# Top-k attention and an MLP mixer on one core: six tiles by DMA in every pair of heads from the ninth, O scaled by ScalarE in every other, GpSimd taking two tiles instead of three in first groups

## The chip, the cores and the metric

The kernel runs on one core of a Trainium2 chip. The metric is the device time in microseconds (us) of one execution; of several runs the median is given.

## What is computed

The inputs are q, k and v, each 8 batches x 8 heads x 576 rows x 64 columns in f32, and the four weights of a mixer block. Cut to what matters:

```python
scores = scale * q @ k.transpose(0, 1, 3, 2)          # 576 x 576 for each batch and head
kth = np.partition(scores, -32, axis=-1)[..., -32:-31]
scores = np.where(scores >= kth, scores, -1e9)        # the 32 largest of each row stay
attn = softmax(scores)
x = (attn @ v) as 8 x 576 x 512                       # heads side by side
h = np.maximum(x^T @ w_tok1, 0) @ w_tok2              # over the rows, 576 -> 256 -> 576
u = x + h^T
out = u + np.maximum(u @ w_ch1, 0) @ w_ch2            # over the columns, 512 -> 1536 -> 512
```

## The kernel before

The work is cut into 32 units. Unit u is a pair of heads: u = 4 b + p for batch b and pair p, counted from 0, so the ninth pair is unit 8. A pair has 2 x 576 rows of scores. They make nine tiles of 128 rows: tiles 0 to 7 are four blocks of 128 rows for each of two heads, and tile 8 holds the last 64 rows of both heads. Tiles 0 to 3 are the first group (g = 0, scores in `SS0`), tiles 4 to 8 the second (g = 1, `SS1`).

For each group VectorE finds the 32nd largest score of every row, which the program calls the selection: `upper` (L461) takes the larger of the two halves of a row, `split4` (L493) splits that into sorted quarters, four rounds of MAX8 (L510) with MATCH_REPLACE8 (L515) between them draw out the largest eight at a time, and `low_round` (L529) ends it. GpSimd does the other half of the comparisons with integer sums and differences (L467): `both_bits`, `lower_bits`, and, for the first few tiles of a group, the "helped" ones, `next_bits` and `next_low`. Those give the smaller of two quarters, which VectorE else computes itself in the second instruction of `split4` (`hx<-hi`). `HELPED = (3, 4)` says how many tiles of each group GpSimd helps; one tile of the first group is left to VectorE.

Then each tile is masked, exponentiated and transposed, in one of two ways:

- The old way: ScalarE writes U, which is above zero where a score is below the 32nd (`below_act`, L622), TensorE transposes E and U together so that U cancels what is to go (`p_tr`, L637 and L640), and ScalarE copies the result into `pt` (`p_ev`, L660, and `ptail_ev`, L680, for the last 64 columns of two tiles).
- By DMA ("turned" tiles): ScalarE writes a mask (`far`, L606), a DMA issued by GpSimd adds it to the scores in place (`sink`, L613), ScalarE exponentiates two tiles at once into `pb` (L587), and SyncE issues two DMA transposes from `pb` into `pt` (`turn`, L618).

`TURNED = (0, 1, 4, 5)` are turned in every unit, and in units 8, 10, ... 28 also tiles 2 and 3 (`SIX`). Units 30 and 31 turn tiles 0 to 3.

When `pt` is full, TensorE forms O = P V for each of the two heads, 25 matmuls in one PSUM bank (`o_mm`, L705). The last column of O is the sum of the weights. VectorE takes its reciprocal (`rden`, L717), and O is scaled into `xb`: the first head by five ScalarE instructions (`o_ev`, L727), the second by one VectorE instruction (`o_ev_dve`, L736). There is one bank for O, so the matmuls of the second head wait until the first is scaled. These steps of unit u fall into the first group of unit u + 2 on VectorE. The mixer of a batch (L747 to L851) runs on TensorE and ScalarE beside the selection of the next units.

A planner sets the order of the instructions on each engine: every step is a task with a duration, a priority and the buffers that it takes and gives back, and `Plan.order` lists the tasks by a simulated time. The priorities come from the table `RANK`, with further entries for how long a wait is to be expected (`den0_wait` to `den3_wait` for the reciprocals, `t_wait` for the transposes). On the chip each engine works through its list in order, and waits for the others by semaphores. In idle stretches of the plan TensorE gets matmuls without use (`spare`, L296, "filling"). Until 80 us of the plan's time they fill 80% of a gap; from then on 1.2 us of each gap (`REST`) is left out first.

Of the kernel before, what the change touches and what calls it, by code (L numbers as in the profile page):

```python
# [17 lines left out]
FIRST_FROM = 30  # L18
HELPED = (3, 4)
FIRST_HELPED = (0, 4)  # L20
DIVIDED = 1
SIX_HELPED = (3, 4)
SIX_DIVIDED = 1
SPARE = 0.8
PARTS = 3
JOINT = 4
PRE_OF = 12
NUB = 2
RANK = {
    "h2_gap": 1409, "out_gap": 376, "begin_l": -8, "den0_wait": 10, "den1_wait": 12, "den2_wait": 40, "den3_wait": 46, "t_wait": 16,  # L30
    "q_wait": 206, "v_wait": 1272, "pre_mm": -2610, "pre_ev": -135, "rest_mm": -250, "early_mm": 106, "early_ev": 625, "begin_a": 1888,
    "begin": 423, "flags": 27, "rush": -2932, "rush5": 53, "rush6": -6233, "load": -205, "qk_tr": -245, "qk_ev": -396, "st_mm": 2015,
    "st_ev": -508, "keep": 443, "h1_mm": -684, "h1_ev": -162, "ut_mm": -1061, "ut_ev": -874, "out_mm": 9433, "out_ev": 3197,
# [4 lines left out]
    "o_ev1": 215, "z_s_mm": -52, "z_s_ev": -3558, "z_st_mm": -3510, "z_st_ev": 198, "z_exp_u": -1825, "z_exp_t": 77, "z_far": 52,  # L38
    "z_below": 305, "z_sink": 591, "z_p_tr": -413, "z_p_ev": -9, "z_pt_tr": 190, "z_pt_ev": 737, "z_o_mm": 142, "z_o_ev": -93,
    "z_h1_mm": -196, "z_h1_ev": -255, "z_ut_mm": -624, "z_ut_ev": -724, "z_h2_mm": 259, "z_h2_ev": 238, "z_h2t_mm": -665,  # L40
    "z_h2t_ev": -1056, "z_out_mm": -903, "z_out_ev": -61, "z_h2_gap": -89, "z_out_gap": -963,
}
SPARE_US = 0.22
LEAD = 3.0
CALM = (7.0, 10.0)
SETTLED = 80.0
REST = 1.2


# [4 lines left out]
class Plan:  # L54
# [25 lines left out]
    def order(self):  # L80
        free = {t.eng: 0.0 for t in self.tasks}
        ready = {e: [] for e in free}
        slots = {r: [None] * n for r, n in self.bufs.items()}
        nxt = {r: 0 for r in self.bufs}
        freed = {r: [LEAD + (r not in self.early)] * n for r, n in self.bufs.items()}
        for t in self.tasks:
            if t.nd == 0:
                ready[t.eng].append(t)
        running, out, now = [], [], 0.0
        left = len(self.tasks)  # L90
        while left:
            done = [x for x in running if x[0] <= now]
            if done:
                running = [x for x in running if x[0] > now]
                for end, t in done:
                    for key in t.rel:
                        i = slots[key[0]].index(key)
                        slots[key[0]][i] = None
                        freed[key[0]][i] = end
                    for s in t.succ:  # L100
                        s.nd -= 1
                        s.ready = max(s.ready, end + (0.0 if s.eng == t.eng else LAG[t.eng] + s.slack))
                        if s.nd == 0:
                            ready[s.eng].append(s)
            for e in free:
                if free[e] > now:
                    continue
                best = None
                shut = any(x[1].port and x[0] > now for x in running)
                for t in ready[e]:  # L110
                    if t.port and shut:
                        continue
                    if t.ready > now or (best is not None and (best.prio, best.seq) < (t.prio, t.seq)):
                        continue
                    n = {}
                    ok = True
                    for r, *_ in t.acq:
                        i = (nxt[r] + n.get(r, 0)) % self.bufs[r]
                        ok = ok and slots[r][i] is None
                        n[r] = n.get(r, 0) + 1  # L120
                    if ok:
                        best = t
                if best is not None:
                    ready[e].remove(best)
                    if e == "PE" and best.dur > 0.0:
                        idle = [
                            (max(freed[r][i], free[e]), r, i)
                            for r in self.banks
                            for i in range(self.bufs[r])
                            if slots[r][i] is None  # L130
                        ]
                        at, r, i = min(idle) if idle else (now, "", 0)
                        n = int((now - at - (REST if at > SETTLED else 0.0)) * SPARE / SPARE_US)
                        if n > 0:
                            out.append((now, (r, i, n, now)))
                    for key in best.acq:
                        r = key[0]
                        slots[r][nxt[r] % self.bufs[r]] = key
                        nxt[r] += 1
                    free[e] = now + best.dur  # L140
                    running.append((now + best.dur, best))
                    out.append((now, best))
                    left -= 1
            times = [x[0] for x in running if x[0] > now]
            times += [t.ready for e in ready for t in ready[e] if t.ready > now]
            if not times:
                if left and not any(x[0] <= now for x in running):
                    raise RuntimeError("the plan is stuck")
                continue
            now = min(times)  # L150
        self.span = now
        return out
# [10 lines left out]
def kernel(  # L163
# [126 lines left out]
    def spare(r, i, n, at):  # L290
        if CALM[0] < at < CALM[1]:
            return
        wide = w1b[:, 0:2, :].rearrange("p a c -> p (a c)") if at > SETTLED else zeros[:, :]
        w = wide.shape[1]
        for _ in range(n * 512 // w):
            nc.tensor.matmul(  # L296
                out=banks[r][i][:, 0:w], lhsT=(identB if at > SETTLED else zeros)[:, :], rhs=wide, start=True, stop=True
            )
# [594 lines left out]
    for b in range(B):  # L893
        for t in range(NS):
            at = (0, 0) if b == 0 else ((2, 1), (3, 1), (3, 1), (4, 1), (4, 1))[t] if b == 1 else (NPAIR * b - 2 + t // 2, t % 2)
# [17 lines left out]
        return "F2" if i in (2, 3) else "F"  # L913

    def six(u):
        return u >= 8 and u % 2 == 0

    def plan_unit(u):
        b, p = divmod(u, NPAIR)
# [31 lines left out]
        kb, kd, selE, keep, nmx, PTd = {}, {}, {}, {}, {}, {}  # L951
        preE = None
        st["last"] = last
        st["helped"] = SIX_HELPED if six(u) and u < FIRST_FROM else HELPED if u else FIRST_HELPED
        st["turned"] = [i for i in (FIRST_FOUR if u >= FIRST_FROM else SIX if six(u) else TURNED) if not (last and i >= 4)]
        whole = (
# [6 lines left out]
        for g in range(2):  # L963
# [36 lines left out]
            n = 4 + g  # L1000
# [116 lines left out]
        oe, oes = None, []  # L1117
        for hh in range(2):
            wide = last and hh
            div = wide or hh >= 2 - (SIX_DIVIDED if six(u) and u < FIRST_FROM else DIVIDED)  # L1120
            O = ("mps" if wide else "O", u, hh)
            om = add("PE", 0.97, V + R("o_mm", hh), lambda hh=hh: o_mm(st, mst, p, hh, last),
                     deps=[wt["v", b, t] for t in range(NS)] + [None if last else oe] + tails + [PTd[i] for i in range(NTILE) if i == 2 * NT or i % 2 == hh],
                     acq=[O], rel=([("PT", u)] if hh else []) + ([("vb", b)] if hh and p == NPAIR - 1 else []))
            r = add("DVE", 0.1, U - 500, lambda hh=hh: o_den(st, hh), deps=[om], acq=[("den", u, hh)],
                    slack=0.0 if last else 0.02 * RANK["den%d_wait" % (u % 4)])
            if div:
                r = add("FREE", 0.0, 0, lambda: None, deps=[r])
                oe = add("DVE", 0.46, U - 500, lambda hh=hh: o_ev_dve(st, mst, hh, p), deps=[r], rel=[O, ("den", u, hh)])
            else:  # L1130
                oe = add("ACT", 0.98, V + R("o_ev", hh), lambda hh=hh: o_ev(st, mst, hh, p), deps=[r],
                         acq=[("Xb", b)] if p == 0 and hh == 0 else [], rel=[O, ("den", u, hh)])
            oes.append(oe)
# [365 lines left out]
```

## Time and profile before

| | before |
|---|---|
| median of 3 runs | 853.81 us (852.57, 853.81, 855.36) |
| time of the profiled execution | 855.04 us |
| its span, from the first instruction to the last | 853.3 us |
| VectorE (DVE) busy | 825.9 us, 97% of the span |
| ScalarE (ACT) busy | 782.6 us, 92% |
| TensorE (PE) busy | 788.8 us, 92% |
| GpSimd (POOL) busy | 661.1 us, 77% |
| mean granted TensorE clock | 0.993 |

A busy share is the time in which an engine had an instruction under way. Instructions on VectorE overlap by some 0.1 us at their ends, so what one costs in a full stream is read from the start of one to the start of the next.

### The profile page before, as it was taken

Reading aid. Unit: us, or ns where it says so; the run is one execution under the profiler, and the core shown is the slowest. Engines: PE = TensorE matmul, PEld = TensorE weight load, DVE = VectorE, ACT = ScalarE, POOL = GpSimd, SP = SyncE. Lnnn points to the kernel's source line nnn. Section 1 sums busy time; section 2 is a strip of 40 time slices with the busy share of each in tenths; the row PEclk is TensorE's granted clock in tenths of the full one; section 3 lists DMA queues with packets and bytes.
Section 4 is the critical chain, followed back from the end, with each engine's and each line's share of the span. In section 5 each row is a group of like instructions: output and inputs, shape, how many; then the busy total and the mean of one; then the engine's idle time right before and its main releaser. Section 6 shows DMA issues by size and latency. Waiting matters only on the chain. (4 is left out here: it accounts for less than half of the span.)

```text
span 853.3 us, 21743 instructions
## 1 busy us (share of the span) xinstructions
PE 788.8 (92%) x7189; PEld 449.1 (53%) x7189; DVE 825.9 (97%) x3895; ACT 782.6 (92%) x1591; POOL 661.1 (77%) x525
## 2 busy tenths in 40 slices
PE   8999988988999899899989999898998999899996
PEld 6766554644554555455545445555544555455552
DVE  7999999999999999999999999999999999999982
ACT  4589998999999999999999999999999999999972
POOL 8788888878778987888797887789778887877600
PEclk9999999999999999999999999999999999999998
DMA  9358976566685786679665786768775697445521
GB/s 139 74 97 155 146 142 116 98 116 103 133 176 101 141 145 145 117 117 164 151 141 92 131 165 131 154 104 142 150 146 122 109 170 155 107 74 125 133 33 59
DMA packets 234408, 107.08 MB, mean 125 GB/s; under 512 B 217136, under 2 KB 219632, under 8 KB 234288
## 3 DMA queue, kind: packets, MB, share of 16 engines
q0 software_dynamic: 51360, 52.70, 35.1%
q1 hardware_dynamic: 181648, 52.56, 31.1%
q8 instruction: 58, 0.95, 0.5%
q14 instruction: 62, 0.51, 0.2%
q10 hardware_dynamic: 1280, 0.36, 0.2%
HBM read 35.78 MB, written 9.44 MB: 53 GB/s over the span
## 5 line engine op out<-in xcount | busy, mean ns | idle before, releaser
L510 DVE MAX8 A<-hx 128x8 f32<-128x72 f32 (+2 forms) x1152 | 271.7, 299 | 0.0
L515 DVE MATCH_REPLACE8 hx<-A,hx 128x72 f32<-128x72 f32 (+1 forms) x864 | 200.2, 247 | 0.0
L467 POOL TENSOR_TENSOR hi<-sum,hi 128x1152 int32<-128x1152 int32 x64 | 188.8, 2950 | 4.9
L467 POOL TENSOR_TENSOR sum<-SS 128x1152 int32<-128x1152 int32 x64 | 188.1, 2940 | 4.0 <-ACT SS L366 1.6
L360 ACT COPY SS<-s 128x512 f32<-128x512 f32 x379 | 169.2, 503 | 8.4 <-PE s L422 7.3
L467 POOL TENSOR_TENSOR top<-hi,top 128x576 int32<-128x576 int32 (+1 forms) x63 | 78.8, 1251 | 124.9 <-DVE hx L493 124.9
L422 PE MATMUL s<-qkT 64*128 64x512 f32 x508 | 167.2, 644 | 7.7 <-ACT SS L360 7.4
L640 PE MATMUL tp<-identN,U 128*128 128x128 bf16 (+1 forms) x665 | 97.9, 221 | 22.1 <-ACT U L622 22.0
L529 DVE MAX8 A<-hi 128x8 f32<-128x296 f32 x288 | 117.4, 460 | 0.1
L606 ACT ACTIVATE fbuf<-SS,kbig 128x576 uint8<-128x576 f32 x150 | 115.2, 804 | 1.7 <-DVE kbig L598 1.7
L622 ACT ACTIVATE U<-SS,A 128x576 bf16<-128x576 f32 x133 | 106.7, 811 | 1.5 <-PE tp L640 1.5
L637 PE MATMUL tp<-identB,E 128*128 128x128 bf16 (+1 forms) x665 | 102.0, 224 | 0.1
L843 PE MATMUL mps<-wc2b,H2T 128*128 128x512 bf16 (+1 forms) x420 | 101.4, 380 | 0.0
L461 DVE TENSOR_TENSOR hi<-SS 128x1152 f32<-128x1152 f32 x64 | 99.6, 1556 | 1.2 <-ACT SS L360 0.5
L587 ACT ACTIVATE pb<-SS,nmax 128x1152 bf16<-128x1152 f32 x75 | 96.4, 1285 | 0.0
L802 PE MATMUL mps<-UT,wc1b 128*128 128x512 bf16 x336 | 83.8, 380 | 8.1 <-ACT H2T L809 6.2
L587 ACT ACTIVATE E<-SS,nmax 128x1728 bf16<-128x1728 f32 (+1 forms) x52 | 82.2, 1581 | 9.3 <-DVE nmax L554 9.0
L637 PEld LDWEIGHTS <-E 128*128 128x128 bf16 (+1 forms) x665 | 64.7, 100 | 43.5 <-issue 31.0
L640 PEld LDWEIGHTS <-U 128*128 128x128 bf16 (+1 forms) x665 | 66.3, 101 | 32.8 <-ACT U L622 28.2
L467 POOL TENSOR_TENSOR hx<-top,hi 128x576 int32<-128x576 int32 (+1 forms) x63 | 79.7, 1265 | 4.8
L422 PEld LDWEIGHTS s<-qkT 64*128 64x128 f32 x508 | 47.4, 185 | 55.6 <-ACT SS L360 29.5
L705 PE MATMUL O<-vb,pt 128*128 128x65 bf16 x1575 | 66.1, 195 | 10.1 <-DVE hx L515 5.6
(159 smaller groups left out, 1531.0 us busy)
## 6 DMA issues: line engine op xcount, KB each, us to landing
SS<-fbuf POOLq DMA_DIRECT2D x75, 576.0 KB, 5.0
qL<-in_q_dram SPq DMA_DIRECT2D x62, 128.0 KB, 3.6
kL<-in_k_dram SPq DMA_DIRECT2D x60, 128.0 KB, 3.3
out_dram<-ob SPq DMA_DIRECT2D x28, 256.0 KB, 3.0
vb<-in_v_dram POOLq DMA_DIRECT2D x32, 128.0 KB, 5.9
pt<-pb SPq DMA_TRANSPOSE x150, 2.9
wc1b<-in_moe_w_ch_dram POOLq DMA_DIRECT2D x4, 384.0 KB, 6.8
wc2b<-in_moe_w_ch_dram POOLq DMA_DIRECT2D x4, 384.0 KB, 7.3
```

Source lines behind the costliest of these rows:

```text
L360: nc.scalar.copy(out=out, in_=in_)
L422: nc.tensor.matmul(out=x[:, :], lhsT=T[rows[hh], 0, t * P : (t + 1) * P], rhs=T[rows[hh], 1, 0:W], start=True, stop=True,)
L467: nc.gpsimd.tensor_tensor(out=out.bitcast(i32), in0=in0.bitcast(i32), in1=in1.bitcast(i32), op=op)
L510: nc.vector.max(A[:, i, at], hx[:, i, 0:w])
L515: nc.vector.match_replace(hx[:, i, 0:w], A[:, i, TOP[r] : TOP[r] + 8], hx[:, i, 0:w], NEG)
L529: nc.vector.max(A[:, i, KTH : KTH + 8], lists["hi"][:, i, :])
L587: nc.scalar.activation(out=x[:, 0:n, 0:S], in_=st["SS", g][:, a : a + n, :], func=AF.Exp, bias=st["nmax", g][:, 0:1])
L606: nc.scalar.activation(out=mask_buf(i)[:, a % 2, :].bitcast(u8)[:, 1 : 2 * S : 2], in_=srow(st, i), func=AF.Relu, bias=st["kbig", g][:, a ...
L622: nc.scalar.activation(out=U[:, :], in_=srow(st, i), func=AF.Relu, bias=kcol(st, i), scale=-1.0)
L637: nc.tensor.matmul(out=out, lhsT=st["E", i][:, cols], rhs=identB[:, :], start=True, stop=False)
L640: nc.tensor.matmul(out=out, lhsT=st["U", i][:, cols], rhs=identN[:, :], start=False, stop=True)
L843: nc.tensor.matmul(out=ps[0:ss, 0:C], lhsT=terms[x][0], rhs=terms[x][1], start=(x == 0), stop=(x == n - 1),)
```

## The change

Every unit from 8 to 29 now turns six tiles; before, only the even ones did. In these units GpSimd helps two tiles of the first group, not three (the second group keeps four). In the even ones of them ScalarE scales both heads of O; in the odd ones VectorE scales the second, as before. The filling matmuls leave out the 1.2 us only from 170 us of the plan's time on, not from 80. And `RANK` has other numbers throughout, so that the planner writes another order on every engine.

```diff
-SIX_HELPED = (3, 4)
-SIX_DIVIDED = 1
+SIX_HELPED = (2, 4)
+SIX_DIVIDED = 0
...
-    "h2_gap": 1409, "out_gap": 376, "begin_l": -8, "den0_wait": 10, "den1_wait": 12, "den2_wait": 40, "den3_wait": 46, "t_wait": 16,
+    "h2_gap": 1359, "out_gap": 186, "begin_l": 673, "den0_wait": 33, "den1_wait": 8, "den2_wait": 12, "den3_wait": 35, "t_wait": 0,
...
+SPARSE = 170.0
...
-                        n = int((now - at - (REST if at > SETTLED else 0.0)) * SPARE / SPARE_US)
+                        n = int((now - at - (REST if at > SPARSE else 0.0)) * SPARE / SPARE_US)
...
     def six(u):
-        return u >= 8 and u % 2 == 0
+        return u >= 8
...
-            div = wide or hh >= 2 - (SIX_DIVIDED if six(u) and u < FIRST_FROM else DIVIDED)
+            div = wide or hh >= 2 - (u % 2 if six(u) and u < FIRST_FROM else DIVIDED)
```

Counted over the whole program: on VectorE 22 instructions `hx<-hi` of 144 columns become such of 2 x 144, and 11 of 31 scalings (`xb<-O,rden`, L736) go. ScalarE has 22 masks `far` more and 22 U fewer, 22 copies `p_ev` and 11 `ptail_ev` fewer, and 55 pieces of `o_ev` more. TensorE has 220 small transposing matmuls fewer and 60 filling matmuls of 512 columns more (221, before 161); between the O of unit 0 and that of unit 4 stand 106, where 58 stood. GpSimd has 11 `sink` more, and 22 pairs `next_bits` and `next_low` on two tiles, not three. SyncE has 22 DMA transposes more.

Three places of the new order matter below. The line numbers after the change are higher by one. The first is VectorE at the start of the first group of unit 12, where the two reciprocals for the heads of unit 10 (`rden`) stand; `hi`, `top` and `hx` are the lists of the selection. Before:

```order
L461 TENSOR_TENSOR hi<-SS_4707 128x4x288
L598 TENSOR_SCALAR kbig<-A 128x5
L493 TENSOR_TENSOR top<-hi 128x576
L493 TENSOR_TENSOR hx<-hi 128x144
L493 TENSOR_TENSOR hx<-top 128x4x72 x2
L510 MAX A<-hx 128x8 x4
L515 MATCH_REPLACE hx<-A,hx 128x72 x4
L717 RECIPROCAL rden<-O_148 128x5
L554 TENSOR_REDUCE nmax<-A 128x1
```

After the change, at the same place:

```order
L462 TENSOR_TENSOR hi<-SS_4704 128x4x288
L599 TENSOR_SCALAR kbig<-A 128x5
L718 RECIPROCAL rden<-O_148 128x5
L494 TENSOR_TENSOR top<-hi 128x576
L494 TENSOR_TENSOR hx<-hi 128x2x144
L494 TENSOR_TENSOR hx<-top 128x4x72 x2
L511 MAX A<-hx 128x8 x4
L516 MATCH_REPLACE hx<-A,hx 128x72 x4
L718 RECIPROCAL rden<-O_148 128x5
L555 TENSOR_REDUCE nmax<-A 128x1
```

The first reciprocal has moved ahead of `split4`, the second to where the first stood (before, it comes after the third round), and `hx<-hi` is on two tiles.

The second place is VectorE at the end of the same group, where the second head of unit 10 is scaled before. Before:

```order
L510 MAX A<-hx 128x8
L717 RECIPROCAL rden<-O_148 128x5
L529 MAX A<-hi 128x8
L520 TENSOR_REDUCE hi<-A 128x2x8
L529 MAX A<-hi 128x8 x3
L736 TENSOR_TENSOR xb_124<-O_148,rden 128x5x64
```

After:

```order
L511 MAX A<-hx 128x8
L530 MAX A<-hi 128x8
L521 TENSOR_REDUCE hi<-A 128x2x8
L530 MAX A<-hi 128x8 x3
L462 TENSOR_TENSOR hi<-SS_4869 128x5x288
```

The scaling is gone, so the last MAX8 of the group stands directly ahead of the `upper` of the second group. In the odd units the scaling is there, but ahead of the first L529 (before, in 22 units of the program it is the last instruction of the group; after the change in none).

The third place is TensorE between the matmuls for the two heads of unit 3, with the filling matmuls (`mps<-w1b,identB`). Before:

```order
L705 MATMUL O_148<-vb_114,pt_121 64x65
L381 MATMUL tp_144<-identF,qL 128x64
L381 MATMUL tp_144<-identF,kL 128x64
L296 LDWEIGHTS identB
L296 MATMUL mps_149<-w1b,identB 128x512
```

After:

```order
L706 MATMUL O_148<-vb_114,pt_121 64x65
L352 MATMUL tp_143<-identF,kL 128x128 x4
L382 MATMUL tp_144<-identF,qL 128x64
L382 MATMUL tp_144<-identF,kL 128x64
L397 MATMUL s_145<-qkT 128x64
L397 MATMUL s_146<-qkT 128x64
```

The filling pair stands seven times in a row there before, and nothing else follows until the second head; after the change more work of unit 6 (L352, L397) and six filling pairs stand between the two heads, and seven further pairs follow the second.

More of the change, by code (lines that the diff above doesn't have):

```diff
@@ L29 @@
 RANK = {
-    "h2_gap": 1409, "out_gap": 376, "begin_l": -8, "den0_wait": 10, "den1_wait": 12, "den2_wait": 40, "den3_wait": 46, "t_wait": 16,
-    "q_wait": 206, "v_wait": 1272, "pre_mm": -2610, "pre_ev": -135, "rest_mm": -250, "early_mm": 106, "early_ev": 625, "begin_a": 1888,
-    "begin": 423, "flags": 27, "rush": -2932, "rush5": 53, "rush6": -6233, "load": -205, "qk_tr": -245, "qk_ev": -396, "st_mm": 2015,
-    "st_ev": -508, "keep": 443, "h1_mm": -684, "h1_ev": -162, "ut_mm": -1061, "ut_ev": -874, "out_mm": 9433, "out_ev": 3197,
[4 rows of a table removed]
[L38 to L41, printed above, removed]
+    "h2_gap": 1359, "out_gap": 186, "begin_l": 673, "den0_wait": 33, "den1_wait": 8, "den2_wait": 12, "den3_wait": 35, "t_wait": 0,
+    "q_wait": 732, "v_wait": 815, "pre_mm": -654, "pre_ev": -600, "rest_mm": -515, "early_mm": -7, "early_ev": -5, "begin_a": 374,
+    "begin": -433, "flags": 477, "rush": -1878, "rush5": -706, "rush6": -3498, "load": -223, "qk_tr": 259, "qk_ev": 123, "st_mm": -7,
+    "st_ev": 131, "keep": 77, "h1_mm": 601, "h1_ev": -122, "ut_mm": 442, "ut_ev": 11, "out_mm": 20918, "out_ev": 410, "h2_mm": -19,
[4 rows of a table added]
+    "z_s_mm": 589, "z_s_ev": 950, "z_st_mm": -162, "z_st_ev": 421, "z_exp_u": -268, "z_exp_t": 172, "z_far": 258, "z_below": 171,
+    "z_sink": -331, "z_p_tr": -317, "z_p_ev": 201, "z_pt_tr": -84, "z_pt_ev": 522, "z_o_mm": 210, "z_o_ev": -36, "z_h1_mm": 111,
+    "z_h1_ev": 945, "z_ut_mm": 372, "z_ut_ev": -47, "z_h2_mm": -59, "z_h2_ev": -5805, "z_h2t_mm": -57, "z_h2t_ev": 18,
+    "z_out_mm": -107, "z_out_ev": -626, "z_h2_gap": -59, "z_out_gap": -961,
 }
```

8 rows, old and new, of the table RANK are left out of this document.

## The prediction

> **What bounds the kernel now.** I read the page's first part, then the window of 200 us in the middle of the program. In a windows row stand the stretch, its length, the busy times of TensorE, its weight loads, VectorE, ScalarE and GpSimd, then granted clock, DMA share and GB/s.
>
> ```profile
> PE 788.8 (92%) x7189; PEld 449.1 (53%) x7189; DVE 825.9 (97%) x3895; ACT 782.6 (92%) x1591; POOL 661.1 (77%) x525
> ```
>
> ```profile
> 400.00:600.00 200.00, 185.74 (x1673) 103.42 (x1670) 199.73 (x967) 194.35 (x401) 163.60 (x127) 1.00 0.72 137
> ```
>
> VectorE is busy for 199.73 of 200 us; ScalarE, next, has 5.65 us to spare. Third, the waits of VectorE between 200 and 790 us (us in total, times, longest):
>
> ```profile
> DVE hi L461 <- ACT SS L360: 0.5, 1, 0.5
> DVE rden L717 <- PE O L705: 0.2, 1, 0.2
> ```
>
> That is 0.7 us in 590. So VectorE's own list sets the time of this stretch: what leaves the list is gained, what is added is lost, and what the other engines do counts only where it makes VectorE wait. Fourth, VectorE's timeline (start, duration, what) over two units:
>
> ```profile
> 386.34 1.34 DVE L461 TENSOR_TENSOR hi<-SS 128x1152 f32<-128x1152 f32 x1
> ...
> 388.39 0.30 DVE L493 TENSOR_TENSOR hx<-hi 128x144 f32<-128x144 f32 x1
> 388.61 0.82 DVE L493 TENSOR_TENSOR hx<-top 128x288 f32<-128x288 f32 x2
> 389.35 0.19 DVE L717 RECIPROCAL rden<-O 128x5 f32<-128x5 f32 x1
> ...
> 395.73 0.48 DVE L736 TENSOR_TENSOR xb<-O,rden 128x320 bf16<-128x320 f32 x1
> 396.12 0.47 DVE L529 MAX8 A<-hi 128x8 f32<-128x296 f32 x1
> 396.58 1.21 DVE L529 MAX8 A<-hi 128x8 f32<-128x296 f32 x3
> 397.83 1.66 DVE L461 TENSOR_TENSOR hi<-SS 128x1440 f32<-128x1440 f32 x1
> ...
> 411.17 1.35 DVE L461 TENSOR_TENSOR hi<-SS 128x1152 f32<-128x1152 f32 x1
> ...
> 421.01 1.21 DVE L529 MAX8 A<-hi 128x8 f32<-128x296 f32 x3
> 422.12 0.49 DVE L736 TENSOR_TENSOR xb<-O,rden 128x320 bf16<-128x320 f32 x1
> 422.51 1.66 DVE L461 TENSOR_TENSOR hi<-SS 128x1440 f32<-128x1440 f32 x1
> ...
> 435.86 1.35 DVE L461 TENSOR_TENSOR hi<-SS 128x1152 f32<-128x1152 f32 x1
> ```
>
> Instructions overlap at their ends, so a cost is the distance from one start to the next. The first unit, from 386.34 to 411.17, takes 24.83 us, the second, to 435.86, 24.69. They differ in where the scaling L736 stands. In the second it is the last of the group: three MAX8 from 421.01 to 422.12 are 0.37 each, L736 to `upper` is 0.39. In the first, `upper` follows the MAX8 directly: three from 396.58 to 397.83 take 1.25, where 3 x 0.37 is 1.11. So `upper` of the second group stalls 0.14 us behind a MAX8, and L736 in between hides that.
>
> **The change, part by part.** *Scalings.* Eleven L736 leave VectorE: 11 x 0.39 = -4.3 us.
>
> *Wider `hx<-hi`.* With two helped tiles VectorE takes 22 instructions of 2 x 144 columns for such of 144. The narrow one costs 388.61 - 388.39 = 0.22. The width of 288 is in the next row: two of them from 388.61 to 389.35 are 0.37 each. Hence 22 x 0.15 = +3.3 us. (Bounds: 0, if the engine's fixed part were all, and 22 x 0.22 = +4.8, if width were all; I take the row with the same width and operation.)
>
> *The stall of `upper`.* Over the program, L736 was last in 22 groups and is now last in none (the second place of the order): 22 x 0.14 = +3.1 us. Bounds: 0, if the order now hides the stall in some other way, and +3.1. I take the upper end, since the second place shows MAX8 and `upper` adjacent.
>
> *ScalarE.* The rows of the groups (busy us, mean ns, idle before) and five pieces of `o_ev` in the timeline:
>
> ```profile
> L606 ACT ACTIVATE fbuf<-SS,kbig 128x576 uint8<-128x576 f32 x150 | 115.2, 804 | 1.7 <-DVE kbig L598 1.7
> L622 ACT ACTIVATE U<-SS,A 128x576 bf16<-128x576 f32 x133 | 106.7, 811 | 1.5 <-PE tp L640 1.5
> L660 ACT ACTIVATE pt<-tp 128x512 bf16<-128x512 f32 x106 | 64.9, 629 | 0.8 <-PE tp L640 0.8
> ```
>
> ```profile
> 417.04 1.09 ACT L727 ACTIVATE xb<-O,rden 128x64 bf16<-128x64 f32 x5
> ```
>
> The eleven odd units swap two U for two masks (22 x (811 - 804) ns, nothing) and lose 22 copies of 0.63, -13.9 us (the eleven smaller `ptail_ev`, which go too, I leave out). The eleven even ones gain five pieces each: 11 x 1.09 = +12.0. Together -1.9 us, with 5.65 of 200 free already, so ScalarE does not become the bound and I cost it at 0. If that cover were gone, the price would be the 1.09 us of an even unit, 11 times.
>
> *GpSimd, DMA, TensorE.* The next rows are the mask's DMA and the transposes:
>
> ```profile
> L613 POOL DMA_DIRECT2D SS<-fbuf x75 | 65.1, 877 | 5.9 <-ACT fbuf L606 5.4 <-ACT pt L664 0.3 <-ACT SS L360 0.2
> ```
>
> ```profile
> SS<-fbuf POOLq DMA_DIRECT2D x75, 576.0 KB, 5.0
> pt<-pb SPq DMA_TRANSPOSE x150, 2.9
> ```
>
> Eleven `sink` of 0.88 are 9.6 us for GpSimd, which is idle for 36.4 of 200 and has one tile of `next_bits` and `next_low` less in 22 groups. SyncE issues 22 transposes more. A tile by DMA is thus 5.0 + 2.9 us on its way after issue, where O is formed more than a unit later; behind these issues on the queues stand loads for later units. TensorE loses 220 transposes and gets 60 fillings. All off VectorE's list: 0. Their cover is the distance to the reciprocals, and if it is gone, the second rival below is the price.
>
> *The reciprocals come earlier.* They wait for O, and behind them the whole list of VectorE waits. In the trace of before (timelines of VectorE and TensorE, next unit):
>
> ```profile
> 440.23 0.18 DVE L717 RECIPROCAL rden<-O 128x5 f32<-128x5 f32 x1
> ```
>
> ```profile
> 441.61 1.05 PE L705 MATMUL O<-vb,pt 128*128 128x65 bf16 x25 [1.08 <-DVE hx L515]
> ```
>
> From the first reciprocal over the scaling to the end of the second head's matmuls are 441.61 + 1.05 - 440.23 = 2.43 us. Before, the second reciprocal stands two rounds behind the first. In the new order of an even unit the second stands at the old place of the first, 440.23 - 435.86 = 4.37 us into the unit (0.15 more with the wider `hx<-hi`), and the first right behind `upper` (1.35) and `kbig`: some 3.0 us apart by estimate from these rows, so 0.6 us of slack are left. The first one stands 3 us earlier than before in the even units; if it waits, the whole list waits with it. Against waiting at the first one speaks that O of that head needs nothing of VectorE. Bounds: -0.2 (the one listed wait of before goes) and 22 x 0.2 = +4.4, if each new pair waits as that one did. I take 0, near the lower end, as 0.6 us are left.
>
> *Filling from 80 to 170 us.* The only large loss of VectorE in the trace after the start lies here (windows; timelines of TensorE and VectorE):
>
> ```profile
> 140.00:145.00 5.00, 3.41 (x35) 1.76 (x33) 5.00 (x34) 4.51 (x12) 4.76 (x4) 1.00 1.00 183
> 145.00:150.00 5.00, 5.00 (x20) 2.01 (x20) 5.00 (x13) 4.00 (x8) 3.89 (x3) 0.54 0.72 143
> ```
>
> ```profile
> 143.00 1.06 PE L705 MATMUL O<-vb,pt 128*128 128x65 bf16 x25 [1.59 <-ACT xb L727]
> ```
>
> ```profile
> 160.54 1.34 DVE L461 TENSOR_TENSOR hi<-SS 128x1152 f32<-128x1152 f32 x1
> 166.50 0.20 DVE L717 RECIPROCAL rden<-O 128x5 f32<-128x5 f32 x1 [1.51 <-PE O L705]
> 186.85 1.35 DVE L461 TENSOR_TENSOR hi<-SS 128x1152 f32<-128x1152 f32 x1
> 212.65 1.33 DVE L461 TENSOR_TENSOR hi<-SS 128x1152 f32<-128x1152 f32 x1
> ```
>
> TensorE idles 1.59 us before 143.00 between the two heads (the third place), the granted clock falls to 0.54, TensorE runs late, and the reciprocal at 166.50 holds VectorE for 1.51 us. The two units take 26.31 and 25.80 us, together 2.6 more than 24.69 + 24.83. After the change more work and filling stand in that gap: -2.6 us, with bounds 0 and -2.6. I take the full loss, because the clock is at 1.00 in the window ahead of the gap and at 0.54 behind it. The Trainium skill ("TensorE: Matmul & The Clock Gate", section "HAM oscillation — how this bites in real kernels") speaks against this term: it counts as harmful only idle gaps longer than about 3.4 us. The 1.59 us here are shorter and are followed by a lower clock, so trace and rule differ; by the rule filling would bring 0, which is the first rival. Its next section, "A second HAM failure mode: psum-queue depth-cycling", lets frequent short gaps do the same, which would go with the row.
>
> *The end.* Behind VectorE's list TensorE is the limit:
>
> ```profile
> 814.00:826.00 12.00, 11.55 (x153) 7.67 (x152) 9.83 (x22) 7.93 (x22) 0.00 (x0) 1.00 0.30 29
> ```
>
> Of 12 us it is idle for 0.45, so hardly more than that can be gained here by another order: between 0 and -0.45 I take -0.3, since VectorE's list at the end stays nearly as it was and only TensorE's changes.
>
> **Sum.** -4.3 + 3.3 + 3.1 + 0 - 2.6 - 0.3 = -0.8. Against the profiled execution's own 855.04 us that is 854.2. The median shown is 853.81, and its runs spread over 2.79 us, about the size of the clock's loss; if the median execution lost less of it than the profiled one, the change gives back less. So 854.2 stands 0.05% above the median. A measurement of this kernel can tell about 0.3%, or 2.6 us, from no change (851.2 to 856.4): I forecast no measurable change.
>
> **The rivals.** *The loss of clock stays or has another cause.* For it: the gap is short, and the other terms touch nothing there. Against it: the order of events in the rows above. The sum without -2.6 is 856.8, slower by 0.35%.
>
> *Slower: VectorE waits at the earlier reciprocals.* One mechanism: in the 22 units from 8 to 29 O of a head is not ready when its reciprocal's turn comes, at 0.2 us a unit as in the row of waits, +4.4, so 858.6. It decides from (856.4 - 854.2) / 22 = 0.10 us a unit. For it: the slack shrinks to 0.6 us, and the transposes come through 7.9 us of DMA. Against it: 0.6 us is not nothing, and in 590 us of before such a wait is listed once.
>
> *Faster: `upper` does not stall.* If the 0.14 us belong to something other than the MAX8 ahead of it, +3.1 falls away: 851.1, a gain of 0.3%. For it: the row of `upper` shows no idle time. Against it: the two units compared above differ by exactly that.
>
> **How the numbers follow.** The forecast has a chance of 0.57, the clock's loss staying 0.14, waits at the reciprocals 0.14, no stall 0.15. The predicted time is the first one's. The range goes from the no-stall case, 851.0, to just above the first rival, 857.2; outside lie the case of waits and part of the spread around the no-stall one, some 0.2. Faster by over 0.3% is the no-stall case, 0.15; slower are both slower rivals, 0.28; within 0.3% the rest, 0.57.
>
> **What the profile after would show.** Units of 24.6 us where both heads are scaled by ScalarE (24.69 - 0.39 + 0.15 + 0.14 = 24.59) and of 24.98 in the odd ones (24.69 + 0.15 + 0.14); MAX8 to `upper` of the second group at 0.51 everywhere; the wide `hx<-hi` at 0.37; granted clock 1.00 from 140 to 155 us and no wait of VectorE near 166; no idle time ahead of L718 (the reciprocal's line then). The forecast is wrong if `rden` waits for O add up to more than 2 us, if the clock falls somewhere again, or if a unit's length is off by over 0.1 us with no wait listed.

## The result: 9.3 us slower, and the profile after

| | before | after |
|---|---|---|
| median of six runs each | 853.43 us (852.57 to 855.36) | 862.69 us (860.18 to 865.96) |
| ratio, 95% interval | | 1.0112 (1.0092 to 1.0131) |
| time of the profiled execution | 855.04 | 864.72 |
| its span | 853.3 | 863.0 |

The change makes the kernel 1.1% slower; the forecast was 854.2 (range 851.0 to 857.2) and no measurable change. Its runs fall into two groups, three at 860.2 to 860.7 and three at 864.7 to 866.0 us; the profiled execution is of the upper group.

The page's first part, after:

```profile
PE 781.1 (91%) x6931; PEld 443.1 (51%) x7017; DVE 828.6 (96%) x3884; ACT 784.4 (91%) x1613; POOL 660.0 (76%) x536
```

VectorE's busy time has grown by 2.7 us, the span by 9.7. VectorE's timeline over an undisturbed even unit (from 517.55) and an odd one (from 542.16):

```profile
517.55 1.38 DVE L462 TENSOR_TENSOR hi<-SS 128x1152 f32<-128x1152 f32 x1
518.88 0.23 DVE L718 RECIPROCAL rden<-O 128x5 f32<-128x5 f32 x1
518.98 0.76 DVE L494 TENSOR_TENSOR top<-hi 128x576 f32<-128x576 f32 x1
519.64 0.47 DVE L494 TENSOR_TENSOR hx<-hi 128x288 f32<-128x288 f32 x1
520.01 0.83 DVE L494 TENSOR_TENSOR hx<-top 128x288 f32<-128x288 f32 x2
522.10 0.20 DVE L718 RECIPROCAL rden<-O 128x5 f32<-128x5 f32 x1
...
527.50 1.24 DVE L530 MAX8 A<-hi 128x8 f32<-128x296 f32 x3
528.84 1.66 DVE L462 TENSOR_TENSOR hi<-SS 128x1440 f32<-128x1440 f32 x1
...
542.16 1.37 DVE L462 TENSOR_TENSOR hi<-SS 128x1152 f32<-128x1152 f32 x1
...
567.22 1.38 DVE L462 TENSOR_TENSOR hi<-SS 128x1152 f32<-128x1152 f32 x1
```

The even unit takes 24.61 us (24.59 were forecast), the odd one 25.06 (24.98). The wide `hx<-hi` costs 520.01 - 519.64 = 0.37, as forecast. Neither early reciprocal waits here. So VectorE's list is nearly what the prediction said; the lost time lies elsewhere. The waits of VectorE from 200 to 790 us, where before 0.7 us were listed in all:

```profile
DVE rden L718 <- PE O L706: 6.0, 3, 5.0
DVE hi L462 <- ACT U L623: 0.5, 1, 0.5
DVE hi L462 <- ACT SS L361: 0.5, 1, 0.5
```

One wait for O took 5.0 us, in unit 15, which is 30.18 us long. It is followed back through five views. First the DMAs issued from 374 to 376.5 us (KB each, median us to landing):

```profile
SS<-fbuf POOLq DMA_DIRECT2D x1, 576.0 KB, 11.8
qL<-in_q_dram SPq DMA_DIRECT2D x2, 128.0 KB, 4.9
vb<-in_v_dram POOLq DMA_DIRECT2D x1, 128.0 KB, 4.3
qL<-in_q_dram SPq DMA_DIRECT2D x1, 32.0 KB, 8.1
pt<-pb SPq DMA_TRANSPOSE x1, 12.0
```

Then the timelines of ScalarE, TensorE and VectorE, with the idle time in front in brackets:

```profile
387.68 1.25 ACT L588 ACTIVATE pb<-SS,nmax 128x1152 bf16<-128x1152 f32 x1 [3.61 <-DMA SS<-fbuf]
```

```profile
389.80 4.05 PE L423 MATMUL s<-qkT 64*128 64x512 f32 x6 [3.85 <-ACT SS L361]
```

```profile
395.52 0.20 DVE L718 RECIPROCAL rden<-O 128x5 f32<-128x5 f32 x1 [5.03 <-PE O L706]
```

And windows of 3.41 us (length; busy PE, PEld, DVE, ACT, POOL; granted clock, DMA share, GB/s):

```profile
384.79:388.20 3.41, 1.16 (x8) 0.33 (x5) 3.41 (x10) 0.52 (x1) 2.29 (x1) 1.00 1.11 172
388.20:391.61 3.41, 1.81 (x4) 0.66 (x4) 2.29 (x6) 3.41 (x7) 0.72 (x1) 0.50 0.54 99
391.61:395.02 3.41, 3.41 (x25) 1.64 (x23) 0.00 (x0) 3.23 (x7) 2.61 (x4) 0.50 1.05 217
```

A mask DMA and a transpose issued at the same time, 375.9 us, take 11.8 and 12.0 us, not 5.4 and 3.0 (the medians); a second transpose, 1.3 us later, takes 11.3. Four loads had been issued in the 2.3 us before. ScalarE stands for 3.61 us with score copies queued behind the waiting exponentiation, so TensorE stands for 3.85. Its clock falls to 0.50 for three windows of 3.41 us, six score matmuls take 4.05 us, O comes late, and VectorE, the engine that sets the time, loses 5.03 us.

### The profile page after: what moved, and what is told of

It reads as the page before. It is cut to its first block, busy times and chain, and to the rows that moved or that the text cites. A ratio compares the mean times of both kernels' runs of the same rounds, so it can differ in the third digit from the quotient of the medians.

```text
span 863.0 us, 21374 instructions
## 1 busy us (share of the span) xinstructions
PE 781.1 (91%) x6931; PEld 443.1 (51%) x7017; DVE 828.6 (96%) x3884; ACT 784.4 (91%) x1613; POOL 660.0 (76%) x536
## 4 chain that ended last, share of the span: by engine, by line
DVE 40%; PE 22%; ACT 14%; issue 5%; DMA 3%; SPq 0%; DVEq 0%; ACTq 0%
DVE A L511 11%; DVE hx L516 9%; DVE hi L462 5%; DVE A L530 5%; PE mps L844 4%; PE s L423 4%; ACT pb L588 4%; DVE hx L494 3%; PE O L706 3%; PE mps L803 3%; DVE top L494 3%; ACT SS L361 2%; ACT fbuf L607 2%; ACT U L623 2%; DMA SS<-fbuf 1%
## 5 line engine op out<-in xcount | busy, mean ns | idle before, releaser
L468 POOL TENSOR_TENSOR top<-hi,top 128x576 int32<-128x576 int32 (+2 forms) x63 | 73.2, 1162 | 106.0 <-DVE hx L494 106.0
L607 ACT ACTIVATE fbuf<-SS,kbig 128x576 uint8<-128x576 f32 x172 | 131.5, 802 | 0.2 <-DVE kbig L599 0.2
L641 PE MATMUL tp<-identN,U 128*128 128x128 bf16 (+1 forms) x555 | 81.1, 220 | 19.5 <-ACT U L623 19.0
L614 POOL DMA_DIRECT2D SS<-fbuf x86 | 73.6, 874 | 32.0 <-ACT fbuf L607 30.8
L803 PE MATMUL mps<-UT,wc1b 128*128 128x512 bf16 x309 | 78.1, 384 | 17.9 <-ACT UT L793 7.4
L638 PE MATMUL tp<-identB,E 128*128 128x128 bf16 (+1 forms) x555 | 85.6, 223 | 0.9 <-ACT SS L361 0.4
L623 ACT ACTIVATE U<-SS,A 128x576 bf16<-128x576 f32 x111 | 84.4, 791 | 0.5
L516 DVE MATCH_VALUE_LOAD hx<-A,hx 128x8 f32 x864 | 82.2, 95 | 0.0
L588 ACT ACTIVATE E<-SS,nmax 128x1728 bf16<-128x1728 f32 (+1 forms) x41 | 67.2, 1642 | 13.0 <-DVE nmax L555 12.9
L706 PEld LDWEIGHTS <-pt 128*128 128x128 bf16 (+1 forms) x1600 | 60.7, 101 | 33.0 <-issue 25.4
L468 POOL TENSOR_TENSOR hx<-top,hi 128x576 int32<-128x576 int32 (+2 forms) x63 | 72.6, 1152 | 4.9
```

The costliest lines, as they stand in the source:

```text
L468: nc.gpsimd.tensor_tensor(out=out.bitcast(i32), in0=in0.bitcast(i32), in1=in1.bitcast(i32), op=op)
L516: nc.vector.match_replace(hx[:, i, 0:w], A[:, i, TOP[r] : TOP[r] + 8], hx[:, i, 0:w], NEG)
L588: nc.scalar.activation(out=x[:, 0:n, 0:S], in_=st["SS", g][:, a : a + n, :], func=AF.Exp, bias=st["nmax", g][:, 0:1])
L607: nc.scalar.activation(out=mask_buf(i)[:, a % 2, :].bitcast(u8)[:, 1 : 2 * S : 2], in_=srow(st, i), func=AF.Relu, bias=st["kbig", g][:, a ...
L638: nc.tensor.matmul(out=out, lhsT=st["E", i][:, cols], rhs=identB[:, :], start=True, stop=False)
L803: nc.tensor.matmul(out=ps[:, 0:W], lhsT=wc1b[:, cc, fc * P : (fc + 1) * P], rhs=mst["UT"][:, cc, 0:W], start=(cc == 0), stop=(cc == NC - 1),)
```

## The clock goes by stretches of 3.41 us

In every profile here the granted clock at any moment is 1.00 or 0.50 (a window's figure is the mean over it), and each stretch of 0.50 in the middle of a program is 3.41, 6.83 or 10.24 us long. A second example needs no late DMA. Unit 10 after, windows and TensorE's timeline:

```profile
255.09:258.50 3.41, 1.38 (x8) 0.48 (x5) 3.41 (x23) 3.41 (x6) 3.33 (x2) 1.00 0.04 9
258.50:261.91 3.41, 3.41 (x15) 1.63 (x14) 3.41 (x12) 2.64 (x8) 3.39 (x6) 0.50 0.44 87
```

```profile
257.64 2.77 PE L803 MATMUL mps<-UT,wc1b 128*128 128x512 bf16 x8 [2.03 <-ACT H2T L810]
```

TensorE is busy for 1.38 of 3.41 us, in its longest gap idle for 2.03, and the next 3.41 us run at 0.50. The table lays such a grid over all fourteen profiles (before, after and the versions below), from the start of a half-clock stretch on, and counts TensorE's busy share in each stretch at full clock between 35 and 830 us:

| busy share of a 3.41 us stretch | stretches | half clock in the next one |
|---|---|---|
| under 0.45 | 22 | 22 |
| 0.45 to 0.52 | 35 | 11 |
| 0.52 to 0.80 | 338 | 7 |
| over 0.80 | 2789 | 0 |

A grid laid a few ns otherwise moves one or two stretches between the rows. The share within a stretch thus tells far more than the length of one gap: in the run with the filling alone (below) five gaps of 1.85 us, at a share of 0.46, were followed by full clock. But it doesn't tell all. Seven stretches with a share of 0.52 and more were followed by half clock, and one of them, from 142.0 us on at 0.71, is the loss in the profile of before on which the prediction's filling term rests. What decides there stays open.

The grid lies otherwise in each execution, so a gap that is cut in two by it can do nothing in one and halve the clock in the next. Near 500 us the changed kernel's two profiles have the same least share of some 3.41 us, 0.48, and the clock falls in one alone. Between 80 and 790 us the places where TensorE is busy for less than half of some 3.41 us number 5 before the change and 14 after it.

## The experiments

**The changed kernel again**, with no edit.

> The changed kernel once more, with a profile. Its six executions fall into two groups, three at 860.2 to 860.7 us and three at 864.7 to 866.0. Theory A (a rare collision of DMAs): the upper group has one long stall, in the profiled execution 5.5 us at the reciprocal of unit 15, behind a mask DMA that took 11.8 us; an execution of the lower group has no mask DMA over 8 us and no wait of VectorE for O over 1 us, and is about 4 to 6 us shorter. Rival (the stall belongs to the order): the mask DMA of unit 15 takes over 11 us again in any execution, and VectorE waits there again for 5 us.

866.22 us, so of the upper group again. The mask DMA near 375.7 took 10.4 us, and VectorE waited 3.6 us for O in unit 15. The two DMAs thus meet again at the same place; but the same profile has half clock near 500 and 690 us too, and 0.7 us lost in unit 20 and 2.4 us in unit 27. The second of these has the same start as in unit 15: a mask DMA issued at 679.6 us took 9.2 us, and ScalarE waited 1.0 us for it. In the first profile the mask of that place, in the same order, took 4.9 us and nothing was lost. Theory A's lower group was not seen here. The rival is right that unit 15 stalls again, with 10.4 and 3.6 us for its 11 and 5.

**Only the filling of the change, on the kernel before.**

```diff
-n = int((now - at - (REST if at > SETTLED else 0.0)) * SPARE / SPARE_US)
+n = int((now - at - (REST if at > SPARSE else 0.0)) * SPARE / SPARE_US)   # SPARSE = 170
```

> The kernel before with only the filling matmuls between 80 and 170 us changed (the 1.2 us left out only from 170 us on). Theory of the prediction: units 6 and 7 take 24.7 and 24.8 us without the half clock from 145 us on, and the median goes down by up to 2.6 us (850.8 to 853). Rival (the clock's loss is of that one execution and mostly absent): within 1 us of before. Second rival: filling delays useful matmuls, slower by over 1 us.

852.70 us (852.00 to 853.51) against 853.25 beside it, ratio 0.9987 (0.9976 to 0.9997): 0.1% faster than before, at the edge of what can be told. The windows that showed the clock's loss:

```profile
140.00:145.00 5.00, 4.53 (x41) 2.51 (x41) 5.00 (x32) 4.58 (x11) 4.82 (x3) 1.00 1.02 185
145.00:150.00 5.00, 5.00 (x48) 2.88 (x47) 5.00 (x13) 5.00 (x11) 3.75 (x3) 1.00 1.12 135
```

TensorE is busy for 4.53 us in the first, not 3.41, and the clock stays at 1.00. Unit 6 takes 24.70 us, not 26.31; unit 7 25.28, not 24.8, since its second `upper` waits 0.5 us as in the trace of before. The forecast's mechanism holds; its 2.6 us were those of an execution that had this loss, and the median gives back 0.55.

**The filling of before, in the changed kernel** (`SPARSE = 80`; 169 filling matmuls of 512 columns, not 221, all other instructions in the same order).

> The changed kernel with the filling matmuls of before (1.2 us left out from 80 us on). If the change's filling is not what costs time, it stays within 1.5 us of the changed kernel's lower group (859 to 862) or gets slower by up to 2.6 us by a half clock near 145 us; if the filling delays units 3 to 9, it is 1 to 2 us faster than 860.

865.69 us (862.48 to 875.98), ratio 1.0180 (1.0111 to 1.0248). Three of its four executions, 862.48 to 867.02, can't be told apart from the changed kernel's; the fourth took 875.98. The profile has half clock at 118, 258, 558 and 749 us. The change's filling isn't what costs time. The profile also settles a point of the run before: from 170 us on its order is that of the changed kernel, but here the mask of unit 15, issued at 375.7 us, took 5.7 us, and unit 15 is 25.06 us long without a wait. So the order brings the DMAs together there, but they aren't slow in each execution.

**Only the new order, on the kernel before** (`RANK` of the change, everything else of before).

> The kernel before with only the new table RANK: the same work on every engine, other order. Theory B (the order costs): units 6 to 11 and 30 show VectorE waiting for score copies of ScalarE as in the changed kernel (0.4 us each in units 6 to 9, 1.1 and 1.8 us in 11 and 30), and the time is 856 to 860. Theory A (the work costs: masks and transposes in odd units): no such waits, 852 to 855.

895.12 us, ratio 1.0477 (1.0449 to 1.0505), far beyond both expectations. The waits of VectorE from 200 to 800 us:

```profile
DVE rden L717 <- ACT SS L360: 14.7, 4, 3.7
DVE rden L717 <- PE O L705: 4.8, 5, 2.6
```

The table can't be judged apart from the work that it orders; so the order's share in the loss stays open in this form, and the next runs keep the order as it is.

**Filling everywhere, in the changed kernel.**

```diff
-SPARSE = 170.0
+SPARSE = 1000.0
```

> The changed kernel with filling matmuls in the whole program as they are up to 170 us (464 of 512 columns, not 221); the order of all other instructions on every engine is the same. Theory C (gaps of TensorE that the plan foresees halve its clock, and then O comes late for the earlier reciprocals): no granted clock under 0.95 near 255, 500 and 690 us, no wait of VectorE for O over 0.3 us outside of unit 15, and 857 to 860. Theory A (only the collision of DMAs near 376 us makes the stalls): the dip at 385 to 400 us and 4 to 5 us of wait in unit 15 stay, 860 to 865. Rival: fillings delay matmuls that VectorE waits for, slower than 863.

856.70 us (855.87 to 858.90), ratio 1.0041 (1.0025 to 1.0057): 6.0 of the 9.3 us are gone, with no instruction moved but fillings. The two windows of unit 15 and unit 10:

```profile
384.79:388.20 3.41, 3.41 (x20) 1.47 (x18) 3.41 (x12) 3.41 (x7) 3.12 (x5) 1.00 0.17 35
...
255.09:258.50 3.41, 2.14 (x10) 0.75 (x10) 3.41 (x27) 3.41 (x4) 3.33 (x2) 1.00 0.00 0
```

No clock under 0.97 is left from 30 to 830 us, no place with TensorE busy for less than 0.63 of 3.41 us, and no wait of VectorE for O is listed from 200 to 790 us. Theory C holds, at slightly less than its 857 to 860. Unit 15 takes 25.26 us; but its mask took only 5.5 us in this execution, so the profile doesn't show what filling does when that mask is slow. The profiled execution, at 858.38 above the median, still loses 1.5 us in unit 12, and this comes from slow DMAs at full clock: a mask and two transposes issued from 298.2 us on took 8.8, 9.0 and 9.1 us, ScalarE waited 2.48 us for them, its score copies and with them GpSimd's `sum` came late, and `upper` beside that `sum` took 2.63 us.

**Small masks, in the changed kernel** (16 of 128 partitions, so most of the masking is left out).

```diff
-out=st["SS", g][:, a - 1 : a + 1, :], in_=mask_buf(i)[:, :, :]
+out=st["SS", g][0:16, a - 1 : a + 1, :], in_=mask_buf(i)[0:16, :, :]
```

> The changed kernel in which each mask DMA moves 16 of the 128 partitions only (most of the masking is left out; instructions and their order are the same). Theory A (masks that collide with transposes and loads make ScalarE wait, TensorE idle, the clock halve and O late): the wait of ScalarE for the mask near 384 us and the 4 to 5 us in unit 15 go, and the time is 857 to 860 in all executions. Theory C (foreseen gaps of TensorE): dips at 255, 500 or 690 us stay and the time goes down by at most the stall of unit 15. Rival (neither: the loss lies in the list and the late score copies): still 860 and more, with units 6 to 11 and 30 long as before and no stall.

858.82 us (858.38 to 859.44), ratio 1.0065 (1.0048 to 1.0082), with little spread. The mask of unit 15 now:

```profile
SS<-fbuf POOLq DMA_DIRECT2D x1, 72.0 KB, 3.9
```

Unit 15 takes 25.06 us, and the wait of ScalarE is gone; half clock at 259 and 747 us stays. So both theories are right in part: the meeting of DMAs makes the largest stall and most of the spread, the gaps of the plan the rest.

**Both together.**

> The changed kernel with both: mask DMAs of 16 partitions (most of the masking is left out) and filling matmuls in the whole program. Filling alone took 6.0 us off the changed kernel, small masks alone 3.9. If the masks' DMAs cost time only through TensorE's clock, the two don't add: 855.5 to 857, as with filling alone. If they also cost time of their own (late masks, late O), they add further: 853 to 855.

856.19 us (855.45 to 857.35), ratio 1.0029 (1.0019 to 1.0039), within the spread of filling alone. Beside filling, the masks' DMAs thus cost 0.5 us in the median. This doesn't show that they cost time only by way of TensorE's clock: unit 12 with filling, above, speaks against it, and so does unit 15 with three helped tiles and filling, below.

**Filling everywhere on the kernel before** (438 filling matmuls, not 161).

> The kernel before with filling matmuls in the whole program (438, not 161), all else in the same order. The kernel with filling to 170 us alone showed no clock under 0.97 any more and 852.7 us, so if filling only works through the clock, nothing is left to gain: 852 to 853.3. If units 10, 14, 18, 22, 26, whose first reciprocal waits 0.2 us for O, wait for a TensorE that is late by fillings, they get longer: up to 856.

852.74 us, ratio 0.9991 (0.9981 to 1.0001), like 214 of them. With no clock to win back, more filling does nothing, good or bad.

**No filling after 80 us on the kernel before** (`REST = 1000`, 13 filling matmuls left, all else in the same order).

> The kernel before without the filling matmuls after 80 us (13 of 161 of 512 columns are left), all other instructions in the same order. Theory C (a 3.41 us stretch in which TensorE is busy for less than about half is followed by half clock, and O then comes late): half clock in several places, waits of VectorE for O of 1 us and more, 855 to 862. Rival (the old order has slack enough, and fillings matter only to the new one): one or two stretches of half clock, but within 1.5 us of before.

873.90 us (873.05 to 875.70), ratio 1.0233 (1.0215 to 1.0250): 20 us slower with 148 useless matmuls fewer, well beyond the 855 to 862 of theory C. The granted clock in 40 slices, and the waits of VectorE from 80 to 790 us:

```profile
PEclk9999877999999899899989999799998999899999
```

```profile
DVE rden L717 <- PE O L705: 17.9, 14, 2.0
```

So the kernel before too stands next to this edge, held off it by its fillings.

**Three helped tiles, in the changed kernel**, without and with filling everywhere.

```diff
-SIX_HELPED = (2, 4)
+SIX_HELPED = (3, 4)
```

> The changed kernel with three helped tiles in the first groups, as before the change, so that hx<-hi is narrow again on VectorE and GpSimd has more to do. By the prediction's term VectorE's list gets shorter by 22 x 0.15 = 3.3 us, even units 24.45 and odd ones 24.90 us, and without other effects the time is 3 us under the changed kernel's (857 to 859.5). Rival: the mask's issue on GpSimd then comes later behind the longer next_bits, masks land later, and stalls take back more than 3 us: 862 and more.

> The changed kernel with filling in the whole program and three helped tiles in first groups. Without clock losses the prediction's term can be seen by itself: hx<-hi at 0.22, not 0.37 us, 22 x 0.15 = 3.3 us off VectorE's list, so 853 to 854 against 856.7 with filling alone. Rival (GpSimd's longer next_bits holds VectorE or the mask DMAs): units 24.7 and over 25.1 us as in the version with three helped tiles without filling, 857 or more.

869.32 us, ratio 1.0173 (1.0123 to 1.0222), and with filling 866.46, 1.0136 (1.0109 to 1.0162): both rivals. `hx<-hi` is narrow again, and yet units get longer. GpSimd and VectorE in unit 17 of the version with filling:

```profile
437.09 2.63 POOL L468 TENSOR_TENSOR sum<-SS 128x1152 int32<-128x1152 int32 x1 [1.25 <-ACT SS L361]
```

```profile
438.58 2.35 DVE L462 TENSOR_TENSOR hi<-SS 128x1152 f32<-128x1152 f32 x1
```

and the same with two helped tiles and filling:

```profile
435.11 2.63 POOL L468 TENSOR_TENSOR sum<-SS 128x1152 int32<-128x1152 int32 x1
```

```profile
437.89 1.34 DVE L462 TENSOR_TENSOR hi<-SS 128x1152 f32<-128x1152 f32 x1
```

Where the score copies come late, GpSimd's `sum` (437.09 to 439.72) lies beside VectorE's `upper`, which then takes 2.35 us, not 1.34. With filling this happens in units 13, 17, 21, 25 and 29, for 5.7 us together. About as much goes to waits for O from 200 to 790 us:

```profile
DVE rden L718 <- PE O L706: 5.9, 5, 3.4
```

Two of them, 1.7 us in unit 15 and 3.4 in unit 23, follow masks that took 10.0 and 10.3 us. In unit 15 the clock is 1.00 throughout: ScalarE waited 1.36 us for the mask, and O came late without half clock. The order on the other engines differs too in these two versions, so the loss isn't put down to the third helped tile itself.

**VectorE scales the second head in even units too**, with filling everywhere.

```diff
-(u % 2 if six(u) and u < FIRST_FROM else DIVIDED)
+(1 if six(u) and u < FIRST_FROM else DIVIDED)
```

> The changed kernel with filling in the whole program, and the second head scaled by VectorE in even units too (11 L736 more). By the prediction's terms VectorE's list grows by 11 x 0.39 = 4.3 us where L736 stands inside the group, and by 11 x (0.39 - 0.14) = 2.8 where it is the last of the group: 859 to 861 against 856.7. Rival (ScalarE's five pieces in even units delay score copies, and without them GpSimd's sums come in time): less than 2 us slower, or faster.

872.27 us, ratio 1.0213 (1.0196 to 1.0230). VectorE in unit 22:

```profile
571.85 1.35 DVE L462 TENSOR_TENSOR hi<-SS 128x1152 f32<-128x1152 f32 x1
579.80 0.49 DVE L737 TENSOR_TENSOR xb<-O,rden 128x320 bf16<-128x320 f32 x1
...
596.85 1.35 DVE L462 TENSOR_TENSOR hi<-SS 128x1152 f32<-128x1152 f32 x1
```

25.00 us against 24.61 with filling alone: a scaling inside the group costs 0.39 us, the term as forecast. Most of the other 11 us come from units 12, 17, 20 and 30, each 1.5 to 4.2 us longer than its neighbours of the same kind or than with filling alone, and from the end (73.7 us from the start of unit 31, not 70.3), with half clock at 311 and 512 us in spite of the fillings. The planner wrote another order there, so they aren't the price of the scalings.

## Why the prediction was wrong

*What bounds the kernel: right, but not all.* VectorE's list sets the time as long as nothing makes it wait. What the prediction missed is that two things close by make it wait: TensorE's clock, by its busy share per 3.41 us, and DMAs that are slow where they meet.

*Scalings, wider `hx<-hi`: right.* 0.39 and 0.37 us were measured.

*The stall of `upper`: right in kind, somewhat larger.* Three MAX8 to `upper` are 528.84 - 527.50 = 1.34 us, where 3 x 0.37 is 1.11: 0.23, not 0.14. The idle time in front of `upper` is in the lines: 0.10 us here (528.84 - 527.50 - 1.24), 0.04 in the prediction's line of before (397.83 - 396.58 - 1.21). In all fourteen profiles it is 0.03 us where `upper` follows a MAX8 directly and 0.10 where the trace has one more waiting instruction of VectorE between them, as in every unit from 10 on after the change (units 6 to 9 are told of below). The rival without a stall fell. The odd units' 0.07 us over the forecast, ten times from unit 11 on, are 0.7 us.

*ScalarE, "so ScalarE does not become the bound and I cost it at 0": this failed in unit 30 alone.* There GpSimd's `sum` waits 0.95 us for ScalarE's score copies, and `upper` meets the late `sum` (2.11 us, not 1.37): 0.7 us with filling and 1.8 without.

*A term that the sum doesn't have.* Units 6 to 9 are some 0.37 us longer than their lists, since VectorE stands ahead of the second `upper`, as here in unit 6:

```profile
172.81 1.66 DVE L462 TENSOR_TENSOR hi<-SS 128x1440 f32<-128x1440 f32 x1 [0.46 <-ACT U L623]
```

Unit 7 had this before the change too, so 1.1 us are new. The view names ScalarE, but a late ScalarE doesn't fit: the idle time is 0.45 to 0.47 us each time, in every profile of the new order, while in the one after the change the instruction that is named ended anywhere from 0.00 to 0.28 us ahead of `upper`. With the new table alone, the same 0.46 us stand in units 6 to 13, and VectorE's own MAX8 is named in some. The cause stays open.

*GpSimd, DMA, TensorE "all off VectorE's list: 0": this step failed.* The chain mask, ScalarE, TensorE, O, reciprocal was counted as covered, and 220 transposes fewer as harmless to an engine with work to spare. The runs show otherwise. The cover of TensorE's clock grew thin: 14 places under half, not 5. Whether the missing transposes or the new order opened them wasn't told apart, since the order alone (895 us) says nothing of it. And masks that meet transposes behind four loads took up to 11.8 us, not 5.0, more than the distance to the reciprocals covers. Filling everywhere takes 6.0 us away (856.7), small masks 3.9 (858.8), both 6.5 (856.2). So the step was worth some 6 us, more than the 22 x 0.2 = 4.4 of the second rival, and in few large pieces: three waits for O in 590 us, the longest 5.0. How much of that 5.0 is the slow mask's and how much the half clock's stays open; in unit 15 with three helped tiles and filling a mask of 10.0 us at full clock cost 1.7, in the changed kernel again one of 10.4 us with half clock 3.6.

*The reciprocals come earlier: no cost by itself.* In undisturbed units neither waits; 0.6 us of slack was enough. The second rival had the right wait and the wrong mechanism: not 0.2 us in each of 22 units, but O late behind slow masks and half clock in a few. Whether later reciprocals would have waited less was not tried; in the kernel before without filling, with the old places, they waited 17.9 us.

*Filling: right in mechanism, too large.* 0.55 us in the median, not 2.6. The first rival fell with the run that filled only this place. The Trainium skill ("TensorE: Matmul & The Clock Gate", section "What's actually happening") gives the clock a free-running window of 3413 ns; the stretches of 3.41 us here agree, and so does their other place in each execution. Its bound for gaps, cited in the prediction, does not: 2.03 us were enough after the change, and 1.59 before it.

*The five 0.2 us waits for O of before* (units 10, 14, 18, 22, 26) went, all five: -1.0, where one was counted in the bound. *The end* changed by nothing: 70.7 us from the start of unit 31 to the end of the span in both.

Put together from the median of before: 853.4 - 0.5 (filling) - 4.3 + 3.3 + 3.1 + 0.7 (odd units) + 1.1 (units 6, 8 and 9) + 0.7 (unit 30) - 1.0 = 856.5, where filling everywhere measured 856.7; with the 6.0 us that filling takes away it is 862.5, where 862.7 was measured.

## What to carry to other kernels

Where one engine's list sets the time, look for what would make it wait. Count for TensorE not the mean busy share but the stretches of 3.41 us in which it is busy for less than about half (33 of the 40 falls of the clock here followed a stretch under 0.52), also where a change takes work from TensorE. For DMAs, look not at the median but at the places where the new order issues several within a few microseconds. Filling matmuls are a cheap first trial: they take away what gaps in TensorE's plan cost, and what stays is to be looked for elsewhere. And a wait that is forecast at a small price per unit can come as a few large ones.

## What had not been expected of the hardware

A mask DMA of 576 KB and a transpose issued at the same time took 11.8 and 12.0 us in one execution and 10.4 and 10.7 in another, against medians of 5.4 and 3.0; at 430.8 us, issued as closely, 5.1 and 7.0. In the twelve profiles with whole masks seven masks took over 9 us. Each of the seven had a transpose issued within 0.11 us of it and four loads in the 2.3 us before; at 430.8 us there was one load, 3.9 us before. The pattern doesn't always do it: the mask at 375.7 us in the run with the filling of before has four loads in the 2.5 us ahead, and took 5.7.

VectorE's first `upper` of a unit stands still for GpSimd's `sum` where that has started first. It took over 1.45 us instead of 1.37 in 51 cases of the fourteen profiles, each with 0.4 us or more of a `sum` beside it, and in all 51 it ended 1.21 to 1.23 us after that `sum`. In the one case where `sum` started later, by 0.11 us, `upper` took 1.36 us and `sum` 3.75, not 2.63.

And 148 useless matmuls made the kernel before 20 us faster.
